# Moving one pair's block sums, a few edge columns and some reciprocals in an attention and Fourier kernel

## The chip, the cores and the metric

The kernel runs on one core of one Trainium2 chip. The metric is the time of one execution on the device, in microseconds, and the figure compared is the median of several executions. The core has five engines that work side by side, each through its own list of instructions in order: TensorE (PE in the profile; PEld is its loading of weights), VectorE (DVE), ScalarE (ACT), GpSimd (POOL) and SyncE (SP), whose list here is the queue of DMA issues. An engine stops at an instruction whose inputs are not there yet, and everything behind it in its list stops too.

## The reference

Two blocks follow each other. The first is attention over four batches, eight heads, 768 tokens and 64 channels, with a narrow local window and one summary key and value for each block of 32 tokens. The second mixes each batch by a two-dimensional Fourier transform, normalises, and runs two dense layers with a ReLU between them.

```python
k_sum = k.reshape(B, H, nb, block, D).max(axis=3)            # block = 32
v_sum = v.reshape(B, H, nb, block, D).mean(axis=3)
scores_l = where(|i - j| < 16, q @ k.T / sqrt(D), -1e9)
scores_s = q @ k_sum.T / sqrt(D) + log(block)
a = softmax(concat(scores_l, scores_s)); x = a @ concat(v, v_sum)   # heads joined: (B, S, 512)

u = x + real(fft(fft(x, axis=1), axis=2))
un = (u - mean(u)) / sqrt(var(u) + 1e-6)                      # over the 512 channels
out = u + relu(un @ w_ch1) @ w_ch2                            # 512 -> 2048 -> 512
```

The two weight matrices arrive as 64-bit words, which the kernel converts itself to 32-bit numbers.

## The kernel before, in words

The change lies in the first 60 us, where batch 0 goes through its attention and its Fourier input is prepared. The later batches run beside the dense layers and are not touched.

Batch 0's attention (`first_attention`) works in four head pairs, numbered 0 to 3. The steps of a pair are these. `turn` brings q and k to a layout with channels on partitions by TensorE transposes (L728), and `place` copies them out of PSUM by ScalarE and VectorE (L738). `key_maxima` takes the block maxima of k on VectorE (L692). `wide_scores` makes the scores in two halves of the tokens: 12 windows of 64 queries against 96 keys (L750), and all queries of the half against the maxima (L754, which is what needs the maxima). `exponentials` is ScalarE's exp (L759), and `masks` multiplies by the window on VectorE. `add_parts` sums the value windows of a pair by blocks of 32 tokens with matmuls (L773) and has ScalarE copy the sums out (L776). `spread_sums` brings them to the partitions of the summary keys by two matmuls (L781) and one broadcast copy (L782). `wide_values` multiplies the exponentials with the values (L789), takes the reciprocal of the sum of each row for the pair's two heads (L793), and divides. VectorE divides both heads of pairs 0 and 1 (L582 is the line of the helper `tt`, which every tensor-tensor operation of VectorE goes through; L585 is GpSimd's `gtt`). In pairs 2 and 3 it divides head 0 only, and ScalarE divides head 1 in six operations (L797).

The loop runs the pairs shifted against each other: while pair g's values are made, pair g + 1 has its scores and pair g + 2 is turned. It begins at g = -1, where only pair 0's scores and pair 1's turning exist. In its last pass (`ends`) there is nothing more to turn. Within `first_attention` the lists of TensorE, VectorE and ScalarE follow the order of the program text. Behind it a planner orders these engines by priorities and by its own estimates, held in part by explicit marks ("issue this behind that"). The DMA issues of SP keep program order here: q and k of pairs 0 and 1, pair 0's value windows, q and k of pair 2, pair 1's values, and so on; a load whose buffer is not free yet holds up all that stand behind it.

PSUM is shared out in two groups of four banks: `attn` for scores and values, `bank` for turned q and k, block sums and the Fourier products.

The Fourier input of batch 0 is folded four times over, so that the matmuls get shorter. `fold_sequence(par, g0, g1)` adds (par 0) or subtracts (par 1) the two halves of the tokens for the channels of pairs g0 to g1 - 1. `mirror_halves(par, hi)` adds and subtracts mirrored channels of one half of the 512. `fold_channels(par)` joins the two halves, and handles the edge columns (0, 128, 256 and 384 of the folded input), which have no mirror partner, by GpSimd. The room of the folded inputs (`early`) is part of a tile called `wide`; the Fourier products of batch 0 are later written by ScalarE (L1339, L1340) into a tile that takes the same place. `zqs` holds column 128 for an extra product. The products `y` (L1334, with L1338 for the extra one) go through the par 0 groups first. Behind the last fold follow on VectorE the sums of the values of batch 1 (`add_later_blocks`) and the conversion of the weights, in which ScalarE has two operations for each block (L1173, L1186).

Of the kernel before, what the change touches and what calls it, by code (L numbers as in the profile page):

```python
# [496 lines left out]
def _main_program(ctx, tc, q, k, v, moe_w_ch1, moe_w_ch2, out):  # L497


    nc = tc.nc  # L500
    B, H, S, D = q.shape
    DM = H * D
# [4 lines left out]
    NP = H // 2  # L507
# [7 lines left out]
    HD = DM // 2  # L515
# [4 lines left out]
    ADD, SUB = ALU.add, ALU.subtract  # L520
# [16 lines left out]
    o = P + 2 * HT * DM  # L537
# [8 lines left out]
    rec = cpool.tile([P, B * NP, 2, NST], FP, name="rec")  # L546
# [20 lines left out]
    def abank(shape, name):  # L567
        return psum.tile(shape, FP, tag="attn", bufs=4, name=name)
# [12 lines left out]
    def tt(out, in0, in1, op):  # L581
        return nc.vector.tensor_tensor(out=out, in0=in0, in1=in1, op=op).ins  # L582

    def gtt(out, in0, in1, op):
        return nc.gpsimd.tensor_tensor(out=out, in0=in0, in1=in1, op=op).ins  # L585
# [67 lines left out]
    def wide_vw(g):  # L653
        return (vw_bufs + [third, vw_bufs[0]])[g].rearrange("p (e n) d -> p e n d", e=2)

    def load_values(b, g):
        if is_wide(b):
            load_wide_values(b, g)
            return
        load_narrow_values(b, g)  # L660

    def load_wide_values(b, g):

        vw, off = wide_vw(g), v[b, 2 * g].offset
        for r0, r1, i0, i1 in ((0, WK, 1, NQ - 1), (W, WK, 0, 1), (0, WK - W, NQ - 1, NQ)):
            for e in range(2):
                fetch(out=vw[r0:r1, e, i0:i1, 0:D],
                      in_=bass.AP(v.tensor, off + (S * e + QB * i0 - W + r0) * D,
                                  [[D, r1 - r0], [QB * D, i1 - i0], [1, D]]))
# [114 lines left out]
    def wide_values(b, g, p, x):  # L784
        vw = wide_vw(g)
        av = [abank([P, NST, D1], f"av_{b}_{g}_{e}") for e in range(2)]
        for n in range(NQ):
            for e in range(2):
                nc.tensor.matmul(av[e][QB * (n % 2):QB * (n % 2 + 1), n // 2, :], p[:, e, n, :], vw[:, e, n, :],  # L789
                                       start=True, stop=True)  # L790
        for e in range(2):
            rc = rec[:, b * NP + g, e]
            nc.vector.reciprocal(out=rc, in_=av[e][:, :, D])  # L793
            xo = x[:, :, P * g + D * e:P * g + D * (e + 1)]
            if e and g > 1:
                for t in range(NST):
                    nc.scalar.activation(out=xo[:, t], in_=av[e][:, t, 0:D], func=AF.Identity, scale=rc[:, t:t + 1])  # L797
                continue
            tt(xo, av[e][:, :, 0:D], rc[:, :, None].to_broadcast([P, NST, D]), ALU.mult)
# [67 lines left out]
    def first_attention():  # L867

        x = x_of[0] = bpool.tile([P, NST, DM], FP, tag="x", bufs=2, name="x_0")
        fold = bpool.tile([P, 7, 2, S2], FP, tag="u", name="fold_0").rearrange("p a k n -> p (a k n)")  # L870
        wt["fold"] = split_fold(0, fold)
        turned = turned_to(0)
        for n in (1, 0):
            for e in range(2):
                turn(0, turned[0], n, e)
        for n in (1, 0):
            place(turned, n, 0, nc.scalar.copy)
            place(turned, n, 1, nc.vector.tensor_copy)
        key_maxima(0)
        load(0, 2)  # L880
        load_values(0, 1)
        load(0, 3)
        load_values(0, 2)
        ps, spread = {}, {}
        for g in range(-1, NP - 1):
            a, n = g + 1, g + 2
            ends = n == NP
            first = score_banks(a, 0)
            ps[a] = apool.tile([P, 2, NQ, QB], FP, tag="p", name=f"p_0_{a}")
            i = n - 1 if ends else max(g, 0)  # L890
            if i not in spread:
                spread[i] = add_parts(i)
            wide_scores(a, 0, first)
            exponentials(ps[a], 0, first)
            if ends:
                spread_sums(n - 1, nc.scalar.copy, *spread[n - 1])
                mirror_halves(0, 0)
            elif g >= 0:
                spread_sums(g, nc.vector.tensor_copy, *spread[g])
            masks(ps[a], 0)  # L900
            second = score_banks(a, 1)
            if not ends:
                turned = turned_to(n)
                for i in ((1, 0), (1, 1), (0, 0), (0, 1))[:3 + (g < 0)]:
                    turn(n, turned[0], *i)
                place(turned, 1, 0, nc.scalar.copy)
                place(turned, 1, 1, nc.vector.tensor_copy if g < 0 else nc.scalar.copy)
                place(turned, 0, 0, nc.scalar.copy)
                if g < 0:
                    place(turned, 0, 1, nc.vector.tensor_copy)  # L910
                key_maxima(n % 2)
            wide_scores(a, 1, second)
            exponentials(ps[a], 1, second)
            if ends:
                mirror_halves(1, 0)
            masks(ps[a], 1)
            if g >= 0 and not ends:
                turn(n, turned[0], 0, 1)
                if g == 1:
                    spread[2] = add_parts(2)  # L920
                place(turned, 0, 1, nc.scalar.copy)
            if g >= 0:
                wide_values(0, g, ps[g], x)
            if g == 1:
                spread_sums(2, nc.scalar.copy, *spread[2])
            if g == 0:
                load_values(0, 3)
                load(1, 0)
                get_tables(0, lambda: load_raw(1))
                load_raw(2)  # L930
                block_sums(1, 0)
                load(1, 1)
                load_raw(4)
                fetch(out=sel, in_=dr["sel"].ap())
                fetch(out=near, in_=dr["near"].ap().rearrange("p (h i) c -> p h i c", h=2))
                fetch(out=half_of, in_=dr["half"].ap())
                fetch(out=mirror, in_=dr["mirror"].ap())
            for par in range(2 if g == 1 else 0):
                fold_sequence(par, 0, 2)
        fold_sequence(0, 2, 3)  # L940
        wide_values(0, NP - 1, ps[NP - 1], x)
        load_values(1, 0)
        keep_busy(3, ps[NP - 1][:, 0].rearrange("p n c -> p (n c)"))
        nc.gpsimd.memset(zqs[0], 0.0)
        fold_sequence(0, 3, NP)
        mirror_halves(0, 1)
        fold_channels(0)
        fold_sequence(1, 2, NP)
        mirror_halves(1, 1)
        fold_channels(1)  # L950

    def fold_sequence(par, g0, g1):

        x, c = x_of[0], slice(P * g0, P * g1)
        tt(early[par][:, :, c], x[:, 0:HT, c], x[:, HT:NST, c], SUB if par else ADD)

    def mirror_halves(par, hi):

        Q, o = DM // 4, HD * hi
        sd, zw = early[par], wt["fold"][:, par]  # L960
        up, down = sd[:, :, o + 1:o + Q], sd[:, :, o + HD - 1:o + Q:-1]
        tt(zw[:, :, o + 1:o + Q], up, down, ADD)
        tt(zw[:, :, o + Q + 1:o + HD], up, down, SUB)

    def fold_channels(par):

        Q = DM // 4
        sd, zw, fg = early[par], wt["fold"][:, par], wt["fold"][:, 2 - 2 * par]
        ends = [sd[:, :, o:o + Q + 1:Q] for o in (0, HD)]
        gtt(zw[:, :, 0:Q + 1:Q], *ends, ADD)  # L970
        gtt(zw[:, :, HD:HD + Q + 1:Q], *ends, SUB)
        nc.gpsimd.memset(fg[:, :, Q:Q + 1], 0.0)
        nc.gpsimd.tensor_copy(out=fg[:, :, 0:1], in_=zw[:, :, 0:1])  # L973
        nc.gpsimd.tensor_copy(out=zqs[0][:, par, :, 0], in_=zw[:, :, Q])
        nc.gpsimd.tensor_copy(out=fg[:, :, HD:HD + 1], in_=zw[:, :, HD:HD + 1])
        nc.gpsimd.tensor_copy(out=fg[:, :, DM - 1:DM], in_=zw[:, :, HD + Q:HD + Q + 1])
        plus, minus = (slice(o + 1, o + Q) for o in (0, Q))
        over, under = (slice(HD + o + 1, HD + o + Q) for o in (0, Q))
        tt(fg[:, :, plus], zw[:, :, plus], zw[:, :, over], ADD)
        tt(fg[:, :, minus], zw[:, :, minus], zw[:, :, under], ADD)  # L980
        tt(fg[:, :, HD + 1:HD + Q], zw[:, :, minus], zw[:, :, under], SUB)
        marks["fold", 0] = tt(fg[:, :, HD + Q:DM - 1], zw[:, :, plus], zw[:, :, over], SUB)

    zqs, fgs = {}, {}
# [834 lines left out]
    for vw in vw_bufs + [third]:  # L1819
        nc.gpsimd.tensor_copy(out=vw[:, :, D].rearrange("p (e n) -> p e n", e=2),  # L1820
                              in_=count[:, None, :].to_broadcast([P, 2, NQ]))
# [126 lines left out]
```

## Time and profile before

| | |
|---|---|
| median of 3 runs | 795.39 us (794.43 to 795.39) |
| profiled execution | 793.74 us, of which the span of the instructions is 791.8 us |
| mean granted TensorE clock | 0.992 |
| busy: PE, DVE, ACT, POOL | 769.0, 536.8, 249.9, 80.9 us |

A row of a time line gives start and duration in microseconds, the engine, the line of the kernel, the operation, output and inputs by the program's names, how many instructions were merged, and in brackets how long the engine stood idle before them and what ended that. Matmuls are pipelined, so a row's end reaches a little into the next row. TensorE's granted clock is given as a share of full speed.

### The profile page before, as it was taken

The numbers are of one execution on the slowest core, as the hardware profiler recorded it, in microseconds if no ns is written. First come the engines' busy times: TensorE is split into PE (matmuls) and PEld (weight loads), VectorE is DVE, ScalarE is ACT, GpSimd is POOL, SyncE is SP. The second block draws the span as 40 slices with busy tenths as digits, with TensorE's granted clock in tenths as the row PEclk, the third lists the DMA queues.
The fourth block names the chain that finished last, engine by engine and source line by source line (L and its number), as shares of the span: only waits on it lengthen the run. The fifth ranks groups of instructions, "written<-read, shape, count | busy, mean of one in ns | idle before, by whom it ended". The sixth has DMA issues, their size and how long they took to land.

```text
span 791.8 us, 14878 instructions
## 1 busy us (share of the span) xinstructions
PE 769.0 (97%) x6020; PEld 580.7 (73%) x6020; DVE 536.8 (68%) x1114; ACT 249.9 (32%) x579; POOL 80.9 (10%) x114
## 2 busy tenths in 40 slices
PE   5989899999999999999999999999999999999997
PEld 3668655445579866688669876688659889889986
DVE  2789999776988747663576726463476887756762
ACT  2764757425536112200126112210116214203300
POOL 1030000000000011200130002300030004201500
PEclk8999999999999999999999999999999999999999
DMA  9799497794865258995354149820614045204001
GB/s 186 169 289 208 122 298 208 252 290 121 223 202 161 74 173 183 260 158 134 120 187 150 41 153 198 216 96 27 252 47 156 27 142 192 94 0 186 2 29 56
DMA packets 135900, 120.35 MB, mean 152 GB/s; under 512 B 94512, under 2 KB 117392, under 8 KB 135824
## 3 DMA queue, kind: packets, MB, share of 16 engines
q1 hardware_dynamic: 134672, 117.05, 53.7%
q0 software_dynamic: 576, 2.10, 0.7%
q8 instruction: 49, 0.80, 0.5%
q10 hardware_dynamic: 576, 0.17, 0.1%
q14 instruction: 27, 0.22, 0.1%
HBM read 95.71 MB, written 23.59 MB: 151 GB/s over the span
## 4 chain that ended last, share of the span: by engine, by line
PE 86%; DVE 7%; ACT 3%; SPq 1%; DMA 1%; issue 1%; DVEq 0%; ACTq 0%
PE ox L1754 18%; PE hx L1461 15%; PE oz L1754 9%; PE hz L1461 7%; PE o L1731 5%; PE oy L1754 4%; PE t L1634 4%; PE hy L1461 3%; PE y L1334 2%; PE f L1634 2%; PE mx L1293 2%; PE sc L809 2%; PE av L845 2%; PE av L850 1%; SPq L562 1%; PE g L1634 1%
## 5 line engine op out<-in xcount | busy, mean ns | idle before, releaser
L1461 PE MATMUL hx<-u,w 128*128 128x384 f32 x384 | 139.4, 491 | 1.8 <-ACT h L1472 1.7
L1461 PEld LDWEIGHTS hx<-u,w 128*128 128x128 f32 x384 | 71.0, 190 | 54.3 <-ACT p L816 4.4
L1754 PE MATMUL oz<-w,s 128*128 128x256 f32 x336 | 81.7, 380 | 0.0
L1754 PE MATMUL ox<-w,s 128*128 128x256 f32 x336 | 80.1, 380 | 0.0
L1754 PE MATMUL ox<-w,h 128*128 128x256 f32 x336 | 79.6, 381 | 0.0
L1754 PEld LDWEIGHTS ox<-w,h 128*128 128x128 f32 x336 | 63.0, 190 | 10.7 <-issue 1.2
L1461 PE MATMUL hz<-u,w 128*128 128x384 f32 x192 | 70.3, 488 | 0.0
L582 DVE TENSOR_TENSOR x<-ox,x 128x256 f32<-128x256 f32 x84 | 35.5, 422 | 51.2 <-PE ox L1754 50.8
L1754 PEld LDWEIGHTS oz<-w,s 128*128 128x128 f32 x336 | 63.3, 190 | 8.9 <-DVE x L582 0.4
L1754 PEld LDWEIGHTS ox<-w,s 128*128 128x128 f32 x336 | 63.0, 190 | 9.2 <-DVE x L582 0.3
L1461 PEld LDWEIGHTS hz<-u,w 128*128 128x128 f32 x192 | 36.2, 190 | 25.2 <-ACT h L1480 0.8
L1472 ACT COPY h<-hx 128x384 f32<-128x384 f32 x24 | 11.5, 478 | 120.9 <-PE hx L1461 120.8
L1731 PE MATMUL o<-w,h 128*128 128x512 f32 x96 | 42.1, 595 | 0.0
L1754 PE MATMUL oy<-w,h 128*128 128x256 f32 x168 | 40.7, 381 | 0.7 <-ACT h L1683 0.7
L1637 ACT COPY f<-t 128x192 f32<-128x192 f32 x52 | 15.8, 303 | 78.3 <-PE t L1634 78.1
L1613 POOL TENSOR_SCALAR h<-h 128x768 f32<-128x768 f32 x12 | 25.4, 2127 | 137.7 <-DVE h L1593 137.7
L585 POOL TENSOR_TENSOR vb<-vb 96x512 f32<-96x512 f32 (+2 forms) x20 | 20.9, 1054 | 179.9 <-DMA vb<-in_v_dram 113.5
L1754 PEld LDWEIGHTS oy<-w,h 128*128 128x128 f32 x168 | 31.5, 190 | 5.9 <-ACT h L1683 1.5
L582 DVE TENSOR_TENSOR x<-oz,x 128x256 f32<-128x256 f32 x42 | 17.8, 423 | 26.7 <-PE oz L1754 26.4
L1461 PE MATMUL hy<-u,w 128*128 128x384 f32 x96 | 34.9, 487 | 0.0
L1731 PEld LDWEIGHTS o<-w,h 128*128 128x128 f32 x96 | 18.0, 190 | 22.1 <-issue 21.0
L1334 PE MATMUL y<-fs,fold 128*128 128x193 f32 x160 | 30.0, 329 | 2.5 <-POOL fold L973 1.8
(241 smaller groups left out, 1322.8 us busy)
## 6 DMA issues: line engine op xcount, KB each, us to landing
w<-dw SPq DMA_DIRECT2D x42, 896.0 KB, 6.0
words<-in_moe_w_ch_dram SPq DMA_DIRECT2D x32, 512.0 KB, 6.3
dw<-w SPq DMA_DIRECT2D x12, 896.0 KB, 7.0
vw<-in_v_dram SPq DMA_DIRECT2D x47, 192.0 KB, 5.7
out_dram<-x SPq DMA_DIRECT2D x23, 256.0 KB, 2.0
vb<-in_v_dram SPq DMA_DIRECT2D x24, 192.0 KB, 7.2
kn<-in_k_dram SPq DMA_DIRECT2D x9, 384.0 KB, 5.6
qn<-in_q_dram SPq DMA_DIRECT2D x9, 384.0 KB, 6.4
```

Source lines behind the costliest of these rows:

```text
L582: return nc.vector.tensor_tensor(out=out, in0=in0, in1=in1, op=op).ins
L585: return nc.gpsimd.tensor_tensor(out=out, in0=in0, in1=in1, op=op).ins
L809: ins = nc.tensor.matmul(ps[h][r:r + 64, i, :], kt[rows, o:o + 64], qt[rows, o:o + BLOCK], start=True, stop=True)
L845: nc.tensor.matmul(av[r][32 * j:32 * (j + 1), t, :], p[rows, h, i - NB2 * h, :], vw[rows, i, :], start=(t == 0), stop=False, skip_group_ch ...
L1293: nc.tensor.matmul(out, y[:, g], table, start=False, stop=True, skip_group_check=True)
L1334: nc.tensor.matmul(y, fgs[b][par][:, st, P * g:P * (g + 1)], fs[par][:, g % 2, st, :], start=(st == 0), stop=(st == n - 1))
L1461: ins = nc.tensor.matmul(ps, w[:, a, kk, :], u[:, r, kk, :], start=start and kk == 0, stop=stop and kk == 1, skip_group_check=True)
L1613: nc.gpsimd.tensor_scalar(out=t, in0=t, scalar1=0.0, scalar2=None, op0=ALU.max)
L1634: marks["two"] = nc.tensor.matmul(o, left(j, a, m), rhs(r, m), start=m in (1, 5), stop=m in (2, 3, 4, 5, 7), skip_group_check=True).ins
L1637: nc.scalar.copy(out={1: f[:, 0], 6: f[:, 1], 7: g}[m], in_=t)
L1731: nc.tensor.matmul(ps, h[:, n, hf, P * t:P * (t + 1)], wt[2, b, j][:, 2 * hf:2 * hf + 2, :], start=(n, hf) == (0, 0), stop=(n, hf) == (NC ...
L1754: nc.tensor.matmul(ps, left[a][:, n, :], wt[2, b, j][:, r, :], start=start and n == 0, stop=stop and n == NC - 1, skip_group_check=True)
```

## The change

The diff makes these edits.

1. In the pass g = -1 `add_parts(0)` is no longer called. Pair 0's block sums are made in the pass g = 0, ahead of the first half of pair 1's scores. Their use, `spread_sums(0)`, stays where it is, in the same pass.
2. `wide_values` takes both reciprocals first, head 1's ahead of head 0's, and then divides head 1 and then head 0.
3. The mirror sums of the lower half for par 1 (`mirror_halves(1, 0)`) move from the last pass, ahead of its second masks, to behind the loop.
4. The par 1 fold of pair 2's channels becomes an operation of its own, ahead of the par 0 fold of pair 3; the par 1 fold behind that covers pair 3 alone.
5. `fold_channels` no longer uses GpSimd for the edge columns, but for clearing one column. VectorE makes them from the folded inputs directly, with four small operations for each par: two sums ahead of the long sums, two differences between the long sums and the long differences.

```diff
@@ wide_values
-        for e in range(2):
+        for e in (1, 0):
+            nc.vector.reciprocal(out=rec[:, b * NP + g, e], in_=av[e][:, :, D])
+        for e in (1, 0):
             rc = rec[:, b * NP + g, e]
-            nc.vector.reciprocal(out=rc, in_=av[e][:, :, D])
             xo = x[:, :, P * g + D * e:P * g + D * (e + 1)]
@@ first_attention
-            i = n - 1 if ends else max(g, 0)
-            if i not in spread:
+            i = n - 1 if ends else g
+            if i >= 0 and i not in spread:
                 spread[i] = add_parts(i)
...
             exponentials(ps[a], 1, second)
-            if ends:
-                mirror_halves(1, 0)
             masks(ps[a], 1)
...
+        mirror_halves(1, 0)
         fold_sequence(0, 2, 3)
         wide_values(0, NP - 1, ps[NP - 1], x)
+        fold_sequence(1, 2, 3)
         load_values(1, 0)
         keep_busy(3, ps[NP - 1][:, 0].rearrange("p n c -> p (n c)"))
         nc.gpsimd.memset(zqs[0], 0.0)
         fold_sequence(0, 3, NP)
         mirror_halves(0, 1)
         fold_channels(0)
-        fold_sequence(1, 2, NP)
+        fold_sequence(1, 3, NP)
         mirror_halves(1, 1)
         fold_channels(1)
@@ fold_channels
-        ends = [sd[:, :, o:o + Q + 1:Q] for o in (0, HD)]
-        gtt(zw[:, :, 0:Q + 1:Q], *ends, ADD)
-        gtt(zw[:, :, HD:HD + Q + 1:Q], *ends, SUB)
+        edge = lambda c: (sd[:, :, c:c + 1], sd[:, :, HD + c:HD + c + 1])
+        tt(fg[:, :, 0:1], *edge(0), ADD)
+        tt(zqs[0][:, par, :, 0:1], *edge(Q), ADD)
         nc.gpsimd.memset(fg[:, :, Q:Q + 1], 0.0)
-        nc.gpsimd.tensor_copy(out=fg[:, :, 0:1], in_=zw[:, :, 0:1])
-        nc.gpsimd.tensor_copy(out=zqs[0][:, par, :, 0], in_=zw[:, :, Q])
-        nc.gpsimd.tensor_copy(out=fg[:, :, HD:HD + 1], in_=zw[:, :, HD:HD + 1])
-        nc.gpsimd.tensor_copy(out=fg[:, :, DM - 1:DM], in_=zw[:, :, HD + Q:HD + Q + 1])
...
         tt(fg[:, :, minus], zw[:, :, minus], zw[:, :, under], ADD)
+        tt(fg[:, :, HD:HD + 1], *edge(0), SUB)
+        tt(fg[:, :, DM - 1:DM], *edge(Q), SUB)
         tt(fg[:, :, HD + 1:HD + Q], zw[:, :, minus], zw[:, :, under], SUB)
```

## The prediction

> **What bounds the kernel now.** I read busy time by stage first, then TensorE's waits by stage. In these rows stand the length, busy time (instructions) of PE, PEld, DVE, ACT and POOL, the granted clock, the DMA share and GB/s; then who waited for whom, in total, how often and longest.
>
> ```profile
> 0.00:92.00 92.00, 78.07 (x1056) 59.47 (x1057) 68.32 (x153) 49.17 (x109) 10.10 (x27) 0.94 0.83 188
> 92.00:791.80 699.80, 690.94 (x4967) 521.26 (x4965) 468.44 (x962) 200.71 (x471) 70.76 (x87) 1.00 0.51 147
> ...
> PE vs L773 <- DMA vw<-in_v_dram: 6.2, 1, 6.2
> PE y L1334 <- POOL fold L973: 1.8, 1, 1.8
> PE av L845 <- ACT vs L835: 1.8, 1, 1.8
> ...
> PE qk L728 <- ACT kt L738: 0.7, 1, 0.7
> ```
>
> From 92 us on TensorE works for 690.94 of 699.80 us: the end is set by a fixed amount of matmul, so whatever lets that stretch begin sooner should come out at the end. Before 92 us it idles 92.00 - 78.07 = 13.9 us. The two longest waits of that stage are the ones that the diff touches: 6.2 us for the first pair's value windows, 1.8 us for GpSimd's edge columns. What else holds the early stage is seen in the time lines (start, duration, engine, operation, count, and in brackets the idle time before it with its releaser), first TensorE's, then VectorE's.
>
> ```profile
> 13.56 1.65 PE L773 MATMUL vs<-vw,wide 96*32 96x128 f32 x24 [6.15 <-DMA vw<-in_v_dram]
> 15.14 2.19 PE L750 MATMUL sc<-qt,kt 64*96 64x64 f32 x24
> 17.25 1.49 PE L754 MATMUL sc<-qt,km 64*32 64x384 f32 x4
> ...
> 21.08 1.24 PE L750 MATMUL sc<-qt,kt 64*96 64x64 f32 x24
> 22.25 0.84 PE L754 MATMUL sc<-qt,km 64*32 64x384 f32 x4
> 24.94 0.41 PE L781 MATMUL vs<-words,wide 128*32 128x128 f32 x2
> ...
> 7.44 1.13 DVE L738 COPY qt<-qk 64x384 f32<-64x384 f32 x2 [0.34 <-PE qk L728]
> 8.60 0.95 DVE L692 TENSOR_REDUCE km<-kt 128x24 f32<-128x768 f32 x1
> 22.65 0.95 DVE L692 TENSOR_REDUCE km<-kt 128x24 f32<-128x768 f32 x1
> 25.39 1.76 DVE L782 COPY vw<-vs 32x1536 f32<-32x1536 f32 x1 [0.72 <-PE vs L781]
> ```
>
> The first pair's block sums (L773) stand ahead of its scores (L750) in TensorE's order, and they alone need the value windows, which come at 13.56. The scores need only the turned q and k, which VectorE finishes at 7.44 + 1.13 = 8.57, and the key maxima, done at 8.60 + 0.95 = 9.55.
>
> **Part 1: block sums behind the first scores.** Nothing is removed; 24 matmuls and one ScalarE copy move from the front of the pass for pair 0 to the front of the pass for pair 1. New start of L750: 8.6. At full clock the 24 take about 1.2 (1.24 with the pipeline's tail), so the four L754 start at 9.8 and take 0.8: end at 10.6 in place of 17.25 + 1.49 = 18.74. Of these 8.1 us, 1.6 (0.95 + 0.65) come from the clock: the row of 15.14 is the same 24 matmuls as that of 21.08, 2.19 against 1.24 us, and L754 of 17.25 takes 1.49 against 0.84. The clock's own rows:
>
> ```profile
> 11.50:12.00 0.50, 0.00 (x0) 0.00 (x0) 0.00 (x0) 0.00 (x0) 0.00 (x0) 0.81 0.93 121
> ...
> 86.50:87.00 0.50, 0.50 (x44) 0.41 (x26) 0.50 (x2) 0.50 (x1) 0.00 (x0) 0.91 0.00 0
> ```
>
> It fell shortly before 12 (0.81 in that half microsecond), some 4.4 us after TensorE fell idle (13.56 - 6.15 = 7.4). In the new order TensorE pauses from 7.4 to 8.6 only, so I take the full clock. The last row warns: near 87 us the clock fell again, after a wait of only 1.8 us (L845 above) among small matmuls. That is the rival "cold" below. The Trainium skill, "TensorE: Matmul & The Clock Gate", section "Part 1: The HAM clock gate (the "warmup" mystery)", says that the throttle sets in after an idle window of some 3.4 us, windows running freely. By that rule a pause of 1.2 us alone costs nothing and the sum stays; the row near 87 us doesn't follow from the pause alone.
>
> What is late next? TensorE's own queue: twelve transposes of pair 1 at 0.13 (three take 0.49 with their tail, a row below), 1.5 us, then pair 0's second half, 1.2 + 0.8, to 14.1. Then the moved block sums, 0.8 at full clock (0.86 with tail, the row of 30.42 below), to 14.9; they want the windows that landed at 13.56, so no wait. They cost 0.8 here, of which 0.7 comes back: the old order stood 0.7 us in the transposes (the last wait above) for a PSUM bank, one of which pair 0's sums held. Pair 1's L750 ends at 16.1. Its L754 want pair 1's maxima, and VectorE, which took 22.65 + 0.95 - 18.74 = 4.86 us from the end of the first L754 to there, has them at 15.5. L754 to 16.9, the two L781 to 17.2, and VectorE's spread copy starts there in place of 25.39: **8.2 us**. ScalarE's copy of the sums now stands ahead of pair 1's exponentials, but these wait for the later L754 anyhow: 0. The step issues no transfer.
>
> From there the order is the old one, 8.2 us sooner, if the loads keep up. They are a queue of their own (SP), and its issues move less:
>
> ```profile
> 11.41 0.49 SPq L562 DMA_DIRECT2D qn<-in_q_dram  x1
> 11.95 4.96 SPq L562 DMA_DIRECT2D vw<-in_v_dram  x6
> 21.66 5.49 SPq L562 DMA_DIRECT2D wide<-in_v_dram  x6
> 30.35 3.46 SPq L562 DMA_DIRECT2D vw<-in_v_dram  x6
> ...
> qn<-in_q_dram SPq DMA_DIRECT2D x1, 384.0 KB, 4.7
> vw<-in_v_dram SPq DMA_DIRECT2D x4, 20.0 KB, 3.4
> ...
> 25.99 0.49 PE L728 MATMUL qk<-ident,qn 128*128 128x128 f32 x3
> 30.42 0.86 PE L773 MATMUL vs<-vw,wide 96*32 96x128 f32 x24
> ```
>
> q of pair 2 is issued at 11.41 and takes 4.7: there at 16.1, wanted at 25.99 - 8.2 = 17.8. Pair 1's values end issuing at 16.9 and land 3.4 later, 20.3, wanted at 30.42 - 8.2 = 22.2. Pair 3's k and q then wait for nothing but the queue (some 1 us), pair 2's values go out at 17.9 in place of 21.66, to 23.4, and pair 3's at 23.4 in place of 30.35. So SP gains 7.0 where the engines gain 8.2; the margins of 1.7 and 1.9 us remain, and I book no loss. The other bound: a load in the denser traffic takes twice the 3.4 of this row, 1.5 us over its margin, and does so for two pairs: 3 us lost.
>
> **Part 2: reciprocals first, one mirror sum and one fold moved into the gaps.** Rows of the seam: VectorE, ScalarE, and VectorE's groups by form (busy, mean ns, idle before).
>
> ```profile
> 46.73 0.56 DVE L582 TENSOR_TENSOR x<-av,rec 128x384 f32<-128x384 f32 x1
> 48.79 0.56 DVE L582 TENSOR_TENSOR wide<-x 128x384 f32<-128x384 f32 x1 [1.40 <-ACT x L797]
> 51.55 0.56 DVE L582 TENSOR_TENSOR wide<-x 128x384 f32<-128x384 f32 x1 [1.40 <-ACT x L797]
> 47.42 1.34 ACT L797 ACTIVATE x<-av,rec 128x64 f32<-128x64 f32 x6 [1.62 <-DVE rec L793]
> L582 DVE TENSOR_TENSOR fold<-wide 128x381 f32<-128x381 f32 x8 | 4.1, 552 | 0.1
> L582 DVE TENSOR_TENSOR wide<-x 128x768 f32<-128x768 f32 x3 | 2.8, 954 | 0.0
> L582 DVE TENSOR_TENSOR wide<-x 128x384 f32<-128x384 f32 x2 | 1.1, 558 | 2.8 <-ACT x L797 2.8
> ```
>
> VectorE twice stands 1.40 us for ScalarE's six divisions (1.34 us), which start only behind the x of the other head. With ScalarE's head taken first they start where that x starts now, 46.73 in place of 47.42: 0.7 sooner, to 48.1. VectorE does the other head to 47.4 and, in the gap, the mirror sums of the odd half that stood ahead of the masks (two of the 552 ns, 1.0 us pipelined) to 48.4. Their old place, ahead of the masks, gives 0 to 1.0 us back, by whether the exponentials and values are there; I take 0. The fold that began at 48.79 begins at 48.4. Pair 3: reciprocals at 48.9, divisions 49.1 to 50.45, and in that gap now a fold of the odd half (0.56). The fold of 51.55 begins at 50.5: **1.05 us**. The odd half's last fold is one pair wide instead of two: 954 - 558 ns = **0.40 us** more. Both reciprocals of pairs 0 and 1 merely change order: 0.
>
> **Part 3: edge columns by VectorE.** Removed: 2 x 6 GpSimd operations (4 sums, 8 copies), so nothing queues behind them there. Added: 2 x 4 VectorE operations of 128x3. No such row exists; the nearest are operations of VectorE on as many elements, shown with two ScalarE rows that close the stage.
>
> ```profile
> 73.54 0.17 DVE L1395 TENSOR_SCALAR stat<-both 128x3 f32<-128x3 f32 x1
> 73.62 0.16 DVE L1396 TENSOR_SCALAR stat<-both 128x3 f32<-128x3 f32 x1
> ...
> 57.21 0.33 ACT L1339 COPY big<-y 128x192 f32<-128x192 f32 x1 [1.65 <-POOL fold L585]
> 63.30 1.15 ACT L1173 ACTIVATE words<-words,rebias 128x1024 int32<-128x1024 int32 x1 [0.82 <-DVE words L1172]
> ```
>
> Each is 0.17 long, but the second, independent of the first, starts 0.08 behind it. So eight cost 8 x 0.08 = 0.64 to 8 x 0.17 = 1.36; the new ones are independent of their neighbours, so I take 0.1 each, 0.8. VectorE's net over parts 2 and 3 is 1.05 + 0.40 - 0.8 = **0.65 us**, and VectorE is the chain here: ScalarE's conversion at 63.30 waits for VectorE's words (0.82), and the Fourier copies stand behind it. The wait of 1.8 us at the first y goes, but is worth nothing by itself: y's copies write a room which the fold's inputs occupy, released at 57.2 by GpSimd's last reading of them. Now VectorE reads last. From 50.5: fold 0.55, mirror 1.0, even half with its four long sums (the same 128x381) and edges 2.3, fold 0.55, mirror 1.0, two edges 0.2, two sums 1.0, two edges 0.2, or 57.3. No gain at that release, 0.1 lost at most. The Trainium skill, "VectorE: DVE Perf Modes", section "The DRAIN you can't avoid", says that the next operation waits until the pipe is empty; the two rows above start 0.08 apart and speak against it here. By it the eight would cost 1.36 and the sum would be 8.3 instead of 8.9.
>
> **Sum.** 8.2 + 0.65 = 8.85, say 8.9 us off. The profiled execution took 793.74 us with a span of 791.8; it would take 784.8. Its time lies 1.65 below the median of 795.39, so the median becomes **786.5**.
>
> **Rivals.**
> Cold: the clock falls in the short pause. For it: the row near 87. Against: it is the only fall behind 19 us in a stage whose mean clock is 0.94 (first row), and the pause is shorter. L750 and L754 take 2.19 + 1.49, ending at 12.3 and not 10.6: 1.7 lost, 788.2.
> Loads bind: SP's queue gives 7.0, and a landing 1 to 3 us later eats the margins; gain 5 to 7.5, so 788 to 790.5. Against: the margins above. The same range holds if the planner, which orders everything behind the first attention by its own estimates, gives back some of the gain before 92.
> Pipe empties between edges: VectorE's net is 1.45 - 1.36 = 0.1, gain 8.3, 787.1.
> Gate stays: the windows still hold TensorE, only parts 2 and 3 count: 794.7, no change. Against: scores use neither them nor the sums.
> Slower: SP's queue stands behind room for raw weights, and what lies behind it comes late.
>
> ```profile
> SPq L562 <- DVE rec L855: 16.5, 1, 16.5
> 97.98 0.42 DVE L582 TENSOR_TENSOR w<-w 128x256 f32<-128x256 f32 x1
> 105.61 1.56 PE L1461 MATMUL hx<-u,w 128*128 128x384 f32 x4
> ```
>
> The second weight block is ready at 97.98 + 0.42 = 98.4, and TensorE takes it up at 105.61: slack 7.2. If VectorE's new order frees the room later, against the rest, by one more wait of 16.5, then 16.5 - 7.2 = 9.3 is lost, and nothing is won. Slower by 0.2% (1.6 us) takes 7.2 + 8.9 + 1.6 = 17.7 or more; at 20 it is 786.5 + 12.8 = 799.3. Against: VectorE frees that room itself, and it is sooner too.
>
> **How the numbers follow.** Sum as worked out, 785 to 787.7: 0.55. Pipe empties: 0.1, inside the same. Cold: 0.1. Loads or planner: 0.15. More than forecast (the slow clock near 87 falls elsewhere, 1.7 us there, to 784): 0.04. Gate stays 0.03, slower 0.03. The range 784.0 to 790.5 leaves out about 0.13. Measurement tells 0.2% (1.6 us) from no change: faster 0.94, same 0.03, slower 0.03.
>
> **What would show it.** Right: the first L750 near 8.6 and at 1.2 us, the spread copy of pair 0 near 17.2, the wait for the value windows gone; ScalarE's divisions some 0.2 us behind TensorE's values, VectorE's 1.40 gaps down to nothing and 0.3; no GpSimd wait at y; the first hidden-layer matmul of 92 us near 83. Wrong: a wait for a load in TensorE before 40 us, a slow clock at 8 to 15 us, edges more than 0.2 us apart, or a new TensorE wait behind 83 us that gives the lead back.

## The result, and the profile after

The changed kernel takes **783.14 us** (median of 4 runs, 782.39 to 786.24) against 795.16 for the kernel before on the same chip: a ratio of 0.9858, 95% interval 0.983 to 0.9885, or 12.0 us less. Measured again beside some of the experiments below it was 784.24, a ratio of 0.9854 (0.983 to 0.9877). The prediction had 786.5, with 784.0 as its low end. Its sum was 8.9 us; some 3 us came from somewhere else. One execution each of `no_front` and `edges_only` below took 1601 us, for a reason that the record does not show: the ratios leave it out, the medians of these two in the table count it.

Busy time by stage, after, cut at the first hidden-layer matmul (the columns are those of the prediction's first fence):

```profile
0.00:78.84 78.84, 74.73 (x1055) 57.25 (x1056) 63.81 (x158) 49.26 (x109) 4.32 (x15) 1.00 0.99 214
78.84:780.60 701.76, 691.36 (x4967) 520.75 (x4965) 470.61 (x966) 200.11 (x471) 70.40 (x87) 1.00 0.52 147
```

That matmul came at 91.98 before. It is 13.1 us sooner, the span 11.2 us shorter; 1.9 us are given back behind it. TensorE's idle time ahead of it fell from 13.9 to 78.84 - 74.73 = 4.1 us, and its busy time there from 78.07 to 74.73, 3.3 us, while the clock rose from 0.94 to 1.00. TensorE's waits in the first 100 us:

```profile
PE hy L1460 <- DVE h L582: 1.5, 1, 1.5
PE warm L1805 <- POOL zeros L1802: 1.4, 1, 1.4
PE sc L750 <- ACT qt L738: 0.8, 1, 0.8
PE mx L1374 <- ACT big L1338: 0.7, 1, 0.7
PE y L1333 <- DVE fold L582: 0.6, 1, 0.6
```

All of the waits shown before are gone (value windows 6.2, GpSimd's fold 1.8, ScalarE's vs 1.8). The first row is new: at 97 us TensorE waits for VectorE, and there 1.5 of the 1.9 us go. The time lines of TensorE's front and of VectorE's seam:

```profile
8.49 1.68 PE L750 MATMUL sc<-qt,kt 64*96 64x64 f32 x24 [0.76 <-ACT qt L738]
10.10 0.84 PE L754 MATMUL sc<-qt,km 64*32 64x384 f32 x4
...
17.43 1.76 DVE L782 COPY vw<-vs 32x1536 f32<-32x1536 f32 x1 [0.69 <-PE vs L781]
...
42.14 0.56 DVE L582 TENSOR_TENSOR wide<-x 128x384 f32<-128x384 f32 x1 [0.28 <-ACT x L798]
42.73 1.17 DVE L582 TENSOR_TENSOR fold<-wide 128x381 f32<-128x381 f32 x4
43.82 1.01 DVE L582 TENSOR_TENSOR fold<-fold 128x381 f32<-128x381 f32 x2
44.75 0.23 DVE L582 TENSOR_TENSOR fold<-wide 128x3 f32<-128x3 f32 x2
44.89 1.01 DVE L582 TENSOR_TENSOR fold<-fold 128x381 f32<-128x381 f32 x2
...
49.51 1.28 DVE L582 TENSOR_TENSOR vb<-vb,vb 96x512 f32<-96x512 f32 x2
```

The spread copy starts 25.39 - 17.43 = 8.0 us sooner. Of the two gaps of 1.40, one is gone and the other is 0.28. Two edge columns together take from 44.75 to 44.89, 0.14. The last row is the first VectorE work behind the folds. Before, that work, the first matmul on the Fourier products (mx) and the first of the hidden layer (hx) stood here:

```profile
58.77 1.28 DVE L582 TENSOR_TENSOR vb<-vb,vb 96x512 f32<-96x512 f32 x2
62.73 0.59 PE L1373 MATMUL mx<-fd,big 128*128 128x256 f32 x2
91.98 0.81 PE L1461 MATMUL hx<-u,w 128*128 128x384 f32 x2
```

VectorE leaves the seam 9.3 us ahead, close to the 8.9 of the sum. The first mx, at 53.41 after, is 9.3 us ahead too, the hidden layer 13.1 and the end 11.2. So in these two profiles the missing gain arises between mx and the hidden layer. There the kernel before has the wait of 1.8 us for vs and some 3.4 us at half clock behind it, and the changed kernel neither.

### The profile page after: what moved, and what is told of

It is laid out like the page before. It is cut to its first block, busy times and chain, and to the rows that moved or that the text cites. A ratio compares the mean times of both kernels' runs of the same rounds, so it can differ in the third digit from the quotient of the medians.

```text
span 780.6 us, 14876 instructions
## 1 busy us (share of the span) xinstructions
PE 766.1 (98%) x6020; PEld 578.0 (74%) x6020; DVE 534.4 (68%) x1123; ACT 249.4 (32%) x579; POOL 74.7 (10%) x102
## 4 chain that ended last, share of the span: by engine, by line
PE 81%; DVE 9%; DMA 5%; ACT 3%; issue 1%; SPq 1%; POOL 0%; DVEq 0%; ACTq 0%; POOLq 0%
PE ox L1753 18%; PE hx L1460 13%; PE oz L1753 9%; PE hz L1460 6%; PE o L1730 5%; PE oy L1753 4%; PE t L1633 4%; DMA words<-in_moe_w_ch_dram 3%; PE hy L1460 3%; PE y L1333 2%; PE f L1633 2%; PE mx L1292 2%; PE sc L810 2%; PE av L846 1%; DVE w L582 1%
## 5 line engine op out<-in xcount | busy, mean ns | idle before, releaser
L1471 ACT COPY h<-hx 128x384 f32<-128x384 f32 x24 | 11.5, 478 | 118.7 <-PE hx L1460 118.7
L1490 ACT ACTIVATE h<-hx 128x384 f32<-128x384 f32 x24 | 11.7, 489 | 62.2 <-PE hx L1460 62.2
```

The source lines that it names most:

```text
L1490: nc.scalar.activation(out=c21, in_=X, func=AF.Relu)
```

## The experiments

Each was timed in five rounds beside the kernel before on the same chip; three chips were used in all, so kernels are compared by the ratio. For size I give what it is of 795 us.

**The parts: front, seam, edges.** `front_only` is edit 1 of the change alone, `seam_only` edits 2 to 4, `edges_only` edit 5; the others are the pairs.

```diff
 front:  i = n - 1 if ends else g;  if i >= 0 and i not in spread: ...      # edit 1
 seam:   reciprocals first; mirror_halves(1, 0), fold_sequence(1, 2, 3) moved   # edits 2-4
 edges:  fold_channels by VectorE                                       # edit 5
```

> Kernel before with edit 1 alone (pair 0's block sums behind its first scores); the order of all other instructions is that of the kernel before. Theory A (three gains: the front, the seam of VectorE, and an order of the planner behind 60 us that changed with the rest): the front alone is worth the lead that the changed kernel has at the spread copy, 25.39 - 17.43 = 8.0 us, so 787.2; TensorE's wait of 1.8 us for a PSUM bank that ScalarE's copy of the scaled sums (vs) frees, and a slow clock behind it, are still there. Rival B (the front was sized too small, the rest is worth nothing): about 783.

> The changed kernel without edit 1: order of all other instructions as in the changed kernel. Theory A: 12.0 - 8.0 = 4.0 us faster than before, 791.2, with ScalarE's vs ahead of the last normalising copy and no wait of TensorE for it. As the prediction summed parts 2 and 3: 0.65 us faster, 794.5. Rival B: 795.

> Before with the reciprocals first, head 1 first, one mirror sum and one fold moved; block sums and edge columns stay as before. Theory A (what lies beyond the front is a VectorE lead that counts all the way to the end): VectorE's folds start some 1.3 us sooner, but GpSimd's edge columns and the 1.8 us wait at the first y stay, so the end is 0.7 to 1.3 us sooner, about 793.9. Rival B (the planner's order behind the first attention decides, not the lead): the values move under 0.3 us, 794.6, or further than the lead, under 793. Rival C (the seam alone is worth nothing, since GpSimd's last reading of the fold's inputs releases the Fourier copies): 794.9.

> Before with the edge columns by VectorE alone; block sums and seam as before. Theory A: eight additions of about 0.12 us lie on VectorE, so the end is 0.5 to 0.9 us later, about 795.6; the wait of TensorE for GpSimd at the first y goes without effect. Rival B (planner's order): the ScalarE copy of the next block sums falls ahead of the normalisation, TensorE's wait of 1.8 us near 86 and the half clock behind it go, and VectorE works ahead through the sums that feed the hidden layer: 1.5 to 2.5 us sooner, about 792.9.

> After without its last part: GpSimd takes the edge columns again. Theory A (VectorE's lead counts, edges are a small cost): front 8.0 and seam 1.3 make 9.3, about 785.6 beside 783.1 of after, because the copy of the block sums is behind the normalisation as before. Rival B (the seam's lead is lost at GpSimd): 786.9, as with the front alone. Rival C (the edges on VectorE are a cost and nothing else): 0.7 below after, 782.4.

> After without the seam: block sums behind the first scores and edge columns by VectorE. Theory A (the edges by VectorE are worth nothing alone, and pay only because they take GpSimd out of the seam's way): 786.9 as the front alone, within 1 us. Rival B (they pay by themselves once the front is shorter, by the order behind the attention): 784 to 785. If A holds, the seam with edges and front is worth 786.9 - 783.7 = 3.2.

> The changed kernel once more, on the same chip as its parts. If the parts add up: front 8.0, and the rest what no_front gave, 2.9, make 10.9, 784.0 to 784.3. If the first result stands: 783.1, 12.0 below before; then about 1 us comes only where both are together.

| kernel | parts | median us | ratio (95%) | us off |
|---|---|---|---|---|
| front_only | front | 786.89 | 0.9901 (0.9887 to 0.9916) | 7.9 |
| seam_only | seam | 796.98 | 1.0027 (1.0013 to 1.0042) | -2.1 |
| edges_only | edges | 794.73 | 0.9994 (0.9977 to 1.0011) | 0.5 |
| no_front | seam, edges | 792.00 | 0.9959 (0.9946 to 0.9972) | 3.3 |
| front_seam | front, seam | 790.07 | 0.9930 (0.9910 to 0.9950) | 5.6 |
| front_edges | front, edges | 785.71 | 0.9891 (0.9868 to 0.9913) | 8.7 |
| after_again | all | 784.24 | 0.9854 (0.9830 to 0.9877) | 11.6 |

The front is worth what was forecast, and its wait for vs is still there, as theory A had it. The seam alone **loses** 2.1 us, and on top of the front 2.3; the edges alone are worth nothing that can be told (0.5 and 0.8); both together win 3.3 without the front and 3.7 with it. So some 5 us lie in the pairing of seam and edges, found twice on separate kernels (without and with the front). Of the expectations for `seam_only` and `front_seam` none held: the loss was not thought of. `no_front` came nearest to its theory A (3.3 of 4.0). `edges_only` lies between its two, and `front_edges`, 0.8 us under `front_only` by the ratio, is nearer to its theory A. `after_again` is where the parts add up, once the pair is counted as one.

Two things other than the lists of the seam are in these differences. The first is the clock: the median of the runs' mean granted clock is 0.995 in `front_seam`, 0.996 in `front_only` and 0.998 in `front_edges` and `after_again`. As 0.001 of 784 us is 0.8 us, up to 2.4 of the 6.0 us between `front_seam` and `after_again` can be clock by this estimate, but hardly any of the 2.9 between `front_edges` and `after_again`. The second is the planner: in the kernels with the edges on VectorE it also orders TensorE's hidden layer, which the diff does not touch, otherwise than in those without, from some 2.5 us into that layer on. No run isolates that.

What the seam changes ahead of the first y is seen in GpSimd's list. Time lines of `front_seam`, GpSimd and then TensorE:

```profile
42.41 1.04 POOL L585 TENSOR_TENSOR fold<-wide 128x6 f32<-128x6 f32 x2 [2.85 <-DVE wide L582]
45.80 1.05 POOL L585 TENSOR_TENSOR fold<-wide 128x6 f32<-128x6 f32 x2 [2.35 <-DVE wide L582]
46.79 0.51 POOL L974 COPY fold<-fold 128x3 f32<-128x3 f32 x1
...
47.36 1.58 PE L1335 MATMUL y<-fs,fold 128*128 128x193 f32 x8 [3.92 <-POOL fold L974]
...
57.93 0.59 PE L1374 MATMUL mx<-fd,big 128*128 128x256 f32 x2
```

The par 0 copies, which the first y needs, could run at 43.45, right behind their own sums. But the planner has put GpSimd's par 1 sums ahead of them, and these wait for VectorE's par 1 input until 45.80. In `front_only` the copies stand directly behind their sums and the same wait is 1.6 us:

```profile
43.87 1.05 POOL L585 TENSOR_TENSOR fold<-wide 128x6 f32<-128x6 f32 x2 [4.30 <-DVE wide L582]
44.86 0.51 POOL L973 COPY fold<-fold 128x3 f32<-128x3 f32 x1
...
45.42 2.91 PE L1334 MATMUL y<-fs,fold 128*128 128x193 f32 x8 [1.63 <-POOL fold L973]
```

**GpSimd's order alone.**

```diff
 # front_seam
-        gtt(zw[:, :, 0:Q + 1:Q], *ends, ADD)
-        gtt(zw[:, :, HD:HD + Q + 1:Q], *ends, SUB)
+        with tc.issue_after(marks["edges", 0]) if par else ExitStack():   # par 0's last copy
+            gtt(zw[:, :, 0:Q + 1:Q], *ends, ADD)
+            gtt(zw[:, :, HD:HD + Q + 1:Q], *ends, SUB)
```

> front_seam with one thing changed: GpSimd's sums of the second half's edge columns are put behind its copies of the first half's, where front_only has them. TensorE's, VectorE's, ScalarE's and SP's orders are those of front_seam. Theory A (the seam cost 3.2 us because GpSimd's in-order queue held the first half's copies behind sums that wait for VectorE's second half): TensorE's wait at the first y falls from 3.9 to 1 us or less, the slow clock behind it goes, and the time falls by 3 to 5 us, to 785.0 to 787.0. Rival B (the VectorE order of the seam is at fault, or the rest of GpSimd's work): 789 to 790.1 as before, the wait stays over 2.5 us.

787.47 us, ratio 0.9915 (0.9896 to 0.9935); TensorE, VectorE, ScalarE and SP keep the order of `front_seam`. TensorE's y, and ScalarE's conversion of the weights:

```profile
44.50 1.47 PE L1336 MATMUL y<-fs,fold 128*128 128x193 f32 x8 [0.75 <-POOL fold L975]
...
55.54 0.89 PE L1336 MATMUL y<-fs,fold 128*128 128x193 f32 x4 [2.48 <-issue]
56.27 0.59 PE L1375 MATMUL mx<-fd,big 128*128 128x256 f32 x2
...
53.40 1.15 ACT L1175 ACTIVATE words<-words,rebias 128x1024 int32<-128x1024 int32 x1 [3.93 <-DVE words L1174]
```

The wait fell from 3.9 to 0.75 as theory A had it, and y starts 2.9 us sooner. Only 1.2 us of this show in the ratio, with intervals that overlap, and the two profiled executions took the same (787.04 and 786.98 us). A second wait, 2.5 us, has taken the first one's place: ScalarE's list still has the conversion ahead of most of the y copies, as in `front_seam`, and it stands there for 3.93 us for VectorE's words while the copies behind it, and the banks they would free, wait. That TensorE waits for these banks is read from the order of the two lists; the trace names no releaser. In the changed kernel y's copies stand ahead of the conversion:

```profile
52.67 0.34 ACT L1338 COPY big<-y 128x192 f32<-128x192 f32 x1
52.89 0.34 ACT L1339 COPY big<-y 128x192 f32<-128x192 f32 x1
54.03 1.15 ACT L1172 ACTIVATE words<-words,rebias 128x1024 int32<-128x1024 int32 x1 [0.80 <-DVE words L1171]
...
53.41 0.59 PE L1372 MATMUL mx<-fd,big 128*128 128x256 f32 x2
```

From each kernel's spread copy (17.05, 17.37 and 17.43) to its first mx (57.93, 56.27 and 53.41) it takes 40.9 us in `front_seam`, 38.9 in `gpsimd_order` and 36.0 after. So on this stretch GpSimd's order, with the half clock that followed its wait in `front_seam` (48.5 to 52), is 2.0 of the 4.9 us; the 2.9 left go with the edges on VectorE and the order of ScalarE and TensorE that the planner makes then. But this stretch does not settle the end. In `front_only` it takes 38.2 us (17.06 to 55.26) and in `front_edges` 39.9 (17.06 to 56.92), and yet `front_edges` is not the slower of the two. That GpSimd's order is what costs the seam its gain is therefore argued from the wait, and not shown by the time.

**ScalarE's order behind the attention.** In the changed kernel the planner also has ScalarE copy batch 1's first block sums (vs) ahead of the normalisation, which before stood first. `after_late` puts the copy back behind; `before_early` puts it ahead in the kernel before.

```diff
 # after_late
+        with tc.issue_after(marks["scaled", 0]) if (b, g) == (1, 0) else ExitStack():
             nc.scalar.activation(out=vs[:, r, 0:D], in_=ps, ...)
 # before_early
+                with tc.high_priority(600) if g == 0 else ExitStack():
                     scale_sums(b, g)
```

> The changed kernel with ScalarE's two vs operations held behind its last normalising copy, as they stood in the kernel before; the order of VectorE is unchanged. Theory A: TensorE waits some 1.8 us again and the clock may fall again. If VectorE sets the pace behind that, 1 to 1.5 us of it reach the end, 784.1 to 784.6; if TensorE does, 3.3 us, 786.4. Rival (the order of vs is of no account): 783.1.

> The kernel before with the vs operations ahead of the last normalising copy; the order of VectorE unchanged. Theory A: the wait of 1.8 us goes and the clock stays full near 87 us; 1 to 1.5 us faster where VectorE sets the pace behind it, 793.7 to 794.2, up to 3.3 us where TensorE does, 791.9. Rival: 795.2, no change.

`after_late` took 784.76 us, ratio 0.9876 (0.9862 to 0.9891), `before_early` 795.06, 1.0007 (0.9996 to 1.0017). The order is worth nothing in the kernel before and at most some 1.7 us after, with intervals that overlap. The wait for vs is back in `after_late` (1.6 us), and the hidden layer begins at 81.35 instead of 78.84; yet VectorE's sums in u begin at 82.04 against 82.05 after, and the span is 781.0 against 780.6. So most of the lead at the hidden layer does not reach the end, and it is not this copy that brought VectorE forward. The planner also ordered TensorE otherwise around 95 us in `after_late`, so the run is not that one change alone.

**Half a clock.** The profiles of one and the same kernel differ. Here are stretches of the kernel before, of `front_only`, and of the changed kernel's second profile, with the granted clock third from the right:

```profile
11.50:19.00 7.50, 5.44 (x55) 3.74 (x56) 0.00 (x0) 0.49 (x2) 0.00 (x0) 0.54 1.02 193
86.50:90.50 4.00, 4.00 (x64) 3.67 (x47) 4.00 (x6) 2.38 (x4) 0.00 (x0) 0.57 0.01 4
```

```profile
45.50:49.00 3.50, 3.50 (x12) 3.50 (x13) 3.47 (x7) 1.80 (x5) 2.63 (x7) 0.51 1.17 275
79.50:83.00 3.50, 3.50 (x23) 3.27 (x22) 3.50 (x5) 1.68 (x3) 0.00 (x0) 0.52 0.00 0
```

```profile
10.00:13.50 3.50, 3.50 (x15) 2.26 (x15) 1.44 (x3) 1.85 (x4) 0.00 (x0) 0.52 1.04 185
98.50:102.50 4.00, 3.98 (x7) 2.21 (x8) 4.00 (x5) 1.30 (x3) 0.00 (x0) 0.57 1.09 273
```

The clock falls to one half for 3.4 us, or a multiple, which costs up to 1.7 us for each 3.4; the kernel before lost 5.1 us so in its profile (two such stretches at 11.5 to 19, one at 86.5), `front_only` and the second profile of after 3.4, the first profile of after nothing. Every one in these rows begins in a wait of TensorE's or within 3 us of its end: waits of 6.2 and 1.8 us, of 1.6 and 2.0, of 0.8 + 0.4 and 1.5. The two profiled runs of the changed kernel took 782.39 and 785.61; the difference, 3.2, is nearly two stretches. In the next runs the waits are filled with work and their ends left where they are.

```diff
 # before_fill (8), after_warm (3): ahead of the first scores, behind pair 0's transposes
+                with tc.issue_after(marks["turned", 0]):
+                    for _ in range(8):
+                        nc.tensor.matmul(first[1], zeros[:, 512:640], zeros[:, 0:S2], start=True, stop=True)
 # front_fill: ahead of the first y
+                    with tc.issue_after(marks["qk", 1, 0]):
+                        for _ in range(4):
+                            nc.tensor.matmul(y, ident, fs[par][:, 0, 0, :], start=True, stop=True)
```

> Before with eight matmuls of 384 columns on zeros (0.70 us each at full clock in after_warm's profile, 5.6 in all) in TensorE's wait for the first pair's value windows, into the bank of the first scores, which are written later; nothing moves on any other engine and the wait's end stays at the windows' landing. Theory A (part of what the front won is clock: the wait lets the clock fall to half in one to three windows of 3.4 us between 9 and 22 us): the clock stays full there, the first scores take 1.24 and not 2.19 us, and the time falls by the 1.6 us that the prediction put into its 8.2, or by up to 3.3 where three windows fell: 791.5 to 793.2. Rival B (the slow clock there is covered by VectorE and ScalarE, or falls anyway, since zeros are not work): 794.5, no change.

> front_only with four matmuls of 193 columns on the identity in TensorE's wait for GpSimd's edge columns at the first y (1.6 us), into y's own bank, which is then written over. The wait's end stays. Theory A (the wait is worth something by the clock that falls behind it, and what the edge columns by VectorE win is that): no half clock at 45 to 50 us, the time falls by up to 1.7 us, to 785.2 to 786.0. Rival B (the wait costs nothing, or the planner's other order from 100 us on decides): 786.9, within 0.5.

> After with three matmuls of 384 columns on zeros in TensorE's pause ahead of the first scores, into the bank of these scores, which then write over it; every other engine's order is that of after. Theory A (the spread of after between 782.4 and 785.6 is the clock, which falls near 10 us in some runs because of that pause): the clock stays full at 8 to 15 us, and the runs lie at 782.3 to 783.0, median 782.6. Rival B (the spread comes from elsewhere): runs between 782.4 and 785.6 as before, median 783.7, or later if the fillers run past the scores' start.

`before_fill`: 791.7 us, ratio 0.9958 (0.9944 to 0.9971), with every other engine's order unchanged. The wait in TensorE's front, its clock, and the scores behind it:

```profile
7.25 5.33 PE L892 MATMUL sc<-zeros 128*128 128x384 f32 x16
13.27 0.98 PE L773 MATMUL vs<-vw,wide 96*32 96x128 f32 x24 [0.69 <-DMA vw<-in_v_dram]
14.19 1.24 PE L750 MATMUL sc<-qt,kt 64*96 64x64 f32 x24
15.35 0.83 PE L754 MATMUL sc<-qt,km 64*32 64x384 f32 x4
...
7.00:20.00 13.00, 11.58 (x110) 7.61 (x110) 5.99 (x11) 4.03 (x10) 1.05 (x4) 1.00 1.12 210
```

The value windows land when they did (13.27, before 13.56), so the block sums begin no more than 0.3 us sooner; but the clock stays at 1.00 and 3.3 us are gone. The mean granted clock is 0.997 to 0.999 in all five runs, against 0.990 to 0.994 in the nine of the kernel before beside them. That is shown then: the wait costs by the clock behind it as well, and 3.3 us can be had without moving the block sums at all. `front_fill` took 785.81, ratio 0.9888 (0.9873 to 0.9903), 1.0 us under `front_only` with overlapping intervals; the half clock at 45.5 is gone from its profile, but the planner also changed VectorE's order from 68 us on and TensorE's from 102. `after_warm` took 783.76, 0.9862 (0.984 to 0.9884): the clock stayed full to 20 us, but the fillers ran until 9.4 us, past the scores' start of 8.5, and the profiled run lost its 1.7 us at 99 us instead. It is no better than the changed kernel, so what spreads that kernel's runs is not settled.

**VectorE's load from 78 us on.**

```diff
-                        (tt if g else gtt)(held[0][:, h], held[0][:, h], near[:, h], ALU.mult)
+                        gtt(held[0][:, h], held[0][:, h], near[:, h], ALU.mult)
```

> After with the second half's neighbour masks of batch 1's second pair (two of 128x384, 1.02 us on VectorE) done by GpSimd as the first pair's are. Theory A (VectorE sets the pace from 78 to 98 us): its sums and the wait of 1.5 us at 97 come 0.9 us sooner, and the end 0.5 to 0.9 us, 782.9. Rival B (GpSimd takes 2 us for the same work and TensorE, or the reordering, waits for that): 783.7 or later.

784.16 us, ratio 0.9867 (0.9845 to 0.9889): no gain. The wait of 1.5 us at 97 is gone, and one of 2.2 us has come up at L846, 20 us ahead of it. The planner changed the order of TensorE, VectorE and ScalarE from 86 us on as well, so whether VectorE sets the pace there stays open.

## Why the prediction was wrong, step by step

**Part 1 was right in size.** Copy 8.0 us sooner for 8.2, end 7.9 by `front_only`. No load held TensorE where the rival saw it: none is among its waits after. VectorE did wait for one in `front_only`, 1.68 us at 57.15 for the small constant half, which the prediction did not list; `after_pool` has such a wait too (1.9 us) and is no slower than the changed kernel (784.16 and 784.24). The clock's share was put at 1.6 for the scores; the block sums (1.65 for 0.87 us) add 0.8, and `before_fill` shows 2.6 us at the spread copy (25.39 to 22.83) and 3.3 at the end.

**"Cold" came true in one profile and not in the other.** The first profile of after has a full clock in the pause, as taken; the second has L754 at half clock:

```profile
8.85 1.23 PE L750 MATMUL sc<-qt,kt 64*96 64x64 f32 x22 [0.40 <-DVE qt L738]
10.00 1.49 PE L754 MATMUL sc<-qt,km 64*32 64x384 f32 x4
...
45.91 1.58 PE L1333 MATMUL y<-fs,fold 128*128 128x193 f32 x8 [0.60 <-DVE fold L582]
```

That run is 1.5 us behind at the first y (45.91 for 44.42), near the 1.7 that the rival priced. So the step's reason, that a pause of 1.2 us is too short, does not hold: here a half clock stands behind pauses of 0.76 and 0.40 us. That the pauses cause it is not shown. The Trainium skill, "TensorE: Matmul & The Clock Gate", section "Part 1: The HAM clock gate (the "warmup" mystery)", whose idle window of some 3.4 us the text took as a minimum for the pause, fits in the length of the slow stretch (3.4 us) and in its free-running phase, which would make it differ from run to run; as a bound on the pause it does not hold here.

**Part 2 was right in size on VectorE, and wrong in sign at the end as long as GpSimd keeps the edges.** The ends of that stretch of VectorE's time line, first in `front_only`, then in `front_seam`:

```profile
17.06 1.76 DVE L782 COPY vw<-vs 32x1536 f32<-32x1536 f32 x1 [0.69 <-PE vs L781]
...
50.44 1.28 DVE L582 TENSOR_TENSOR vb<-vb,vb 96x512 f32<-96x512 f32 x2
```

```profile
17.05 1.76 DVE L782 COPY vw<-vs 32x1536 f32<-32x1536 f32 x1 [0.69 <-PE vs L781]
...
48.87 1.28 DVE L582 TENSOR_TENSOR vb<-vb,vb 96x512 f32<-96x512 f32 x2
```

From the spread copy to the first work behind the folds VectorE takes 50.44 - 17.06 = 33.4 us in `front_only` and 48.87 - 17.05 = 31.8 in `front_seam`: 1.56 won, 1.45 forecast. Yet the end came 2.3 us later. The wait of 3.92 us for GpSimd and the clock are what the record offers for that.

**Part 3 is the step that failed.** It booked the edge columns as a cost of 0.8 and the 1.8 us wait at the first y at nothing, because VectorE "is the chain here". The cost was about 0.6 (twice 0.14 ahead of the long sums, 1.17 for 1.03, and twice 0.15 between them), and 0.26 net of a wait for GpSimd that also goes (after 49.51 - 17.43 = 32.08, `front_seam` 31.82). So VectorE's net is 1.3 and not 0.65. The Trainium skill's rule that the next operation waits for an empty pipe ("VectorE: DVE Perf Modes", section "The DRAIN you can't avoid") does not show in these additions either: two take 0.14 together. That section of the Trainium skill itself lets an operation start earlier where nothing holds it, which the prediction left out. But the large error is the other one. The release of y *was* worth nothing in the kernel before (`edges_only`, 0.9994), and the forecast of that was right; it did not ask what it is worth once part 2 has been done. With the seam moved, TensorE waits 3.9 us for GpSimd at the first y, and the edges by VectorE win 6.0 us (`front_seam` to `after_again`), where minus 0.8 was booked. Seam and edges together gave 3.3 to 3.7 us for 0.65: that is the miss of 3 us. VectorE's 1.3 accounts for some 0.65 of it. By which path the other 2 to 2.4 us reach the end stays open: GpSimd's wait, the planner's orders behind it and the clock all differ between these kernels.

**The range's low end** rested on one mechanism, "the slow clock near 87 falls elsewhere", at 0.04. That clock did stay full in the first profile, and in the second it fell twice elsewhere: this part is luck of the run. The planner was a rival on the losing side only (788 to 790.5); here its other orders came with a gain, though no run shows how much of it they are.

Of the signs named: scores at 8.5 (in 1.68 us, where 1.2 was named), the copy at 17.4, the gaps, no GpSimd wait at y held; ScalarE's divisions start at 38.60, 0.2 us behind VectorE's reciprocals at 38.37. The hidden layer came at 78.84, not 83, and the new wait behind it did give some back.

## What to carry to other kernels

Price edits that touch the same engine's list together and not one by one: a part that is worth nothing alone can be what lets another part pay. When an engine off the critical path feeds one on it, look at the order of its list after the edit, since a planner may put work that waits ahead of work that doesn't. Where a planner reorders what lies behind, a lead at one point of the trace is not yet a lead at the end. And count TensorE's waits of one to two microseconds at their length plus up to 1.7 us of half clock, and see whether a few matmuls in the wait save that before moving anything.

## What the runs showed of the hardware that was not expected

Waits of 1.5 to 2 us, and once a pause of 0.8 and one of 0.4 us close together, were followed by 3.4 us at half clock in some runs and not in others. `seam_only` had a full clock from 84 to 92 us, with the same 1.8 us wait for vs behind which it was halved in the kernel before:

```profile
84.00:92.00 8.00, 6.22 (x227) 5.25 (x226) 7.59 (x20) 5.19 (x10) 0.47 (x1) 1.00 0.02 4
```

What decides between them is open; the place in a running window is a guess that these runs do not test. Matmuls on zeros kept the clock at 1.00 through a wait of 6 us (`before_fill`). With those on the identity no half clock followed the wait at y, in the one profile of `front_fill`.
